# Repaired positions of instruction blocks, ones and loads in the planner, and 64x64 join and U products for the first two groups

## The chip, the cores and the metric

The kernel runs on one core of a Trainium2 chip. The metric is the device time of one launch in microseconds (us), all inputs starting in HBM and the output ending there. The core's engines work in parallel, each through its own list of instructions in order: TensorE (PE; its weight loads are shown apart as PEld), VectorE (DVE), ScalarE (ACT), GpSimd (POOL) and SyncE (SP), which here only issues DMAs. [...]

## The reference

Two stages follow each other. The first is a delta-rule attention over 768 tokens, for 4 batches of 8 heads of 48 features; the second is a gated product on its 3072 x 384 result, without a nonlinear function.

```python
k_n = k / (np.linalg.norm(k, axis=-1, keepdims=True) + 1e-06)
for t in range(S):
    y[:, :, t] = einsum('bhd,bhde->bhe', q[:, :, t], state)
    v_old = einsum('bhde,bhd->bhe', state, k_n[:, :, t])
    state = state + beta_t * einsum('bhd,bhe->bhde', k_n[:, :, t], v[:, :, t] - v_old)
x = y.transpose(0, 2, 1, 3).reshape(B * S, H * D)
out = ((x @ w_a) * (x @ w_b)) @ w_out
```

## The kernel before

**Attention.** The 768 tokens are cut into 24 chunks of 32 (c0 to c23) and six groups of four chunks. Partition p holds token p % 32 of one of four heads, so a "head" in what follows is one of four bands of 32 partitions, and q counts eight such sets: 32 heads in all. For every group there are three parts:

- `prep(g)` squares and sums the keys on ACT and DVE (`sqf`, `ss`, `nm`, `dc`), forms the products of keys with keys and queries on PE (`ga`, 32 matmuls per chunk, tile `bank<-rawb`), copies the key half on ACT for groups 0 and 1 (tile `tt`, there called `kks`), and scales and masks it on DVE (`b`, `at`). It also sums the squares of v and q on ACT (`sqf<-vnb`, `sqf<-rawb`), from which a power of two for the output is made (`sc`).
- `solve(g)` inverts, on DVE, a triangular 32x32 matrix per head, column by column (`tmp<-b,b` and `b<-b,tmp`). For groups 0 and 1 (`HALVES`) it inverts only the two diagonal 16x16 blocks, in 15 such pairs, and PE joins them: 32 matmuls per chunk (`b,tt`, to be called the first join product), a scaled copy on ACT (`wr`), one transposing matmul against the unit matrix (`b,mk`) and 32 more (`wr,xn`, the second join product). ACT copies the result to `tt`.
- `steps(g)` runs through the chunks in turn: the state (`S_ps`) is copied to `sh` (ACT), keys and queries are multiplied with it (`sh,rawb`), DVE subtracts from v (two results `f`, one for even and one for odd heads), PE forms U with the inverse (`f,tt`, 32 matmuls; for c0 it reads v itself, `vnb,tt`), ACT copies it (`u`), and PE updates the state (`S_ps<-u,knb`) and finishes the output rows (`u,at`), which ACT and DVE scale, transpose and split into two f16 halves (`y`, `yt`, `xb`).

Each step of a chunk needs the state of the one ahead, so this is one long chain.

**The gated product** ("MoE" in the code) takes 256 tokens and one of twelve blocks of 128 hidden features at a time: 18 f16 matmuls (`xb,wh`), a copy `a`, a product `g`, two halves `ghl`, and six matmuls with `wo`. A unit of this is the filler that keeps PE busy for most of the span. Its weights come packed; `weights(p)` unpacks a block with three DVE operations (`wh<-late`, `late<-wh`), takes a power of two from its square sum (`sw`), and makes high and low halves. For the first four blocks the low halves are made on PE (`wh,zi` and `wh,neg`), for the rest on DVE.

**What sets the order.** Nothing runs in the order in which the code names it. `Plan` records every operation, and `order()` (lines 413 to 443) lists them by a simulated schedule (`pack`, line 265), with costs in nanoseconds from `price` (line 154); `issue` (line 451) then writes the engines' lists. Into PE's list it puts matmuls on a tile of ones that nobody reads ("fills", line 455) where the plan has PE idle in the first 60 us (`UNTIL`). The plan also models that PE's instructions come in blocks of 256 (`fetch`, line 398): the next block is asked for when one is entered, and comes 3.5 us later, or 5 us while a DMA is under way (`LOADED`). A product of f32 counts as four instructions (two weight loads and two matmuls), one of f16 as two (`op.words`, line 218). The plan before starts counting at block position 0.

**Loads.** SP issues all loads in one queue. Five kinds come first (`EARLY`, line 44). The later ones (`NEXT`, line 45) are held back: POOL copies one element of an earlier tile into the target, so the load waits until the earlier one has landed (line 1056). Names: k (`knb`) and v (`vnb`) are keys and values of two chunks, r (`rawb`) keys and queries laid by feature, b the two small tables beta and masks (`bt`, `mk`), w a weight block (`late`, or `wh` for the third).

**PSUM banks.** Six tiles `bank` are leased by the plan; the last of them serves only the fills until 60 us. ACT and DVE never read a bank at the same time: their reads of one bank follow each other in the planned order.

Of the kernel before, what the change touches and what calls it, by code (L numbers as in the profile page):

```python
# [43 lines left out]
EARLY = [(0, "k"), (0, "b"), (2, "k"), (0, "r"), (2, "r")]  # L44
NEXT = [(0, "v"), (2, "v"), (0, "w"), (1, "w"), (4, "k"), (2, "w"), (4, "r"), (4, "v")]
# [15 lines left out]
class Plan:  # L61
# [92 lines left out]
    def price(eng, name, outs, ins, kw):  # L154
# [36 lines left out]
    def add(self, eng, fn, name, args, kw):  # L191
# [15 lines left out]
        if eng == "SP":  # L207
# [4 lines left out]
            op.move = max(n / 330.0, 20.0)  # L212
# [52 lines left out]
    def pack(self, pri, back=False):  # L265
# [13 lines left out]
        fill = {}  # L279
# [3 lines left out]
        while len(done) < n:  # L283
# [23 lines left out]
            while can[e] and i is None:  # L307
                i = heapq.heappop(can[e])[1]
                if ops[i].words and not back:
                    slip = self.fetch(t, ops[i].words, ops[i].dur if warm else ops[i].cold, pos, come, dma)[0]  # L310
                    if slip > 1.0:
                        heapq.heappush(wait[e], (t + slip, i))
# [29 lines left out]
            if o.words and not back:  # L342
                _, pos, come = self.fetch(t, o.words, o.dur if warm else o.cold, pos, come, dma)
            if e == "PE" and not back:

                if kept:
                    f, took, many = max(free[e], self.SINCE), self.IDLE * (1 if warm else 2), 0
                    while f + took <= t:
# [3 lines left out]
                        took = self.IDLE * (1 if warm else 2)  # L352
                        use, f, many = use + took, f + took, many + 1
                    fill[i] = many
                    if many:
                        f0 = max(free[e], self.SINCE)
                        _, pos, come = self.fetch(f0, 4 * many, f - f0, pos, come, dma)
# [36 lines left out]
    MOVE = (900.0, 1100.0)  # L394
    LOADED = (3500.0, 5000.0)
    IDLE, SINCE, UNTIL = 440.0, 1500.0, 60e3
# [54 lines left out]
    def issue(self, tc):  # L451
        with tc.manual_schedule():
            for i in self.order():
                for _ in range(self.fill.get(i, 0)):
                    self.nc.tensor.matmul(  # L455
                        self.pool[-1][:, 0:256],
                        self.idle,
                        self.idle.unsqueeze(1).broadcast_to([P, 2, P]),
                        start=True,
                        stop=True,  # L460
                        skip_group_check=True,
                    )
# [5 lines left out]
def tile_kernel(ctx, tc, kqt, kn, vn, beta, w, masks, out):  # L468
# [32 lines left out]
    ttr = ring(cst, "tt", 8, [P, 8, 32], F32)  # L501
    wr = ring(cst, "wr", 2, [P, 8, 16], F32)
# [62 lines left out]
    xnt = one("xn", [P, 512])  # L565

# [68 lines left out]
    ats, tts, kks, nms, gnats, zs, vsum = {}, {}, {}, {}, {}, {}, []  # L635
# [23 lines left out]
    acc = [one(f"acc{i}", [P, DM]) for i in range(4)]  # L659

    loaded, whole = set(), set()

    def target(c, what):
        t = {"w": lambda: slots[c].bitcast(F32), "k": lambda: knp(c)[:, 0], "v": lambda: vnp(c)[:, 0], "r": lambda: rawp(c)[:, 0]}
# [18 lines left out]
    def prep(g):  # L683
# [32 lines left out]
        for ci, c in enumerate(chs):  # L716
# [13 lines left out]
            if HALVES[g]:  # L730
                kks[c] = ttr()
                A.copy(kks[c], ga[:, :, 0:32])
# [49 lines left out]
    def solve(g):  # L782
# [35 lines left out]
        for ci, c in enumerate(chs):  # L818
            tts[c] = ttr()
            if HALVES[g]:  # L820
                wp = att()[:, 0:128].rearrange("p (q t) -> p q t", t=16)
                with plan.group():
                    for q, h4, _, _ in heads():
                        T.matmul(
                            wp[tok(h4), q],
                            kks[c][tok(h4), q],
                            XT[tok(h4), 16:32, ci * 8 + q],
                            start=True,
                            stop=True,
                            skip_group_check=True,  # L830
                        )
# [332 lines left out]
```

## Time and profile before

| what | value |
|---|---|
| time, median of 3 runs | 655.7 us (655.66 to 656.97) |
| profiled execution | 655.28 us |
| its span, first to last instruction | 653.3 us |
| mean granted TensorE clock | 0.986 |
| busy: PE, PEld, DVE, ACT, POOL | 632.7, 540.8, 406.4, 271.3, 19.8 us |
| fills on PE (line 455) | 64 matmuls, shown as 128, 33.8 us |
| first matmul of the gated product | 78.59 us from the span's start |

A matmul of f32 stands in the trace as two matmuls and two weight loads; the profile's counts are of these. Busy time of an engine is the time that any of its instructions covers, so 32 overlapping small matmuls count once. In rows of the timeline the columns are start in us, duration in us, engine, line, operation, output and inputs, shape, count, and in brackets the idle time ahead of it and what ended it. In rows of the windows they are the stretch, its length, then busy time and (count of instructions) for PE, PEld, DVE, ACT and POOL, then PE's granted clock, the DMA engines' busy share, and GB/s.

### The profile page before, as it was taken

The page shows a single profiled execution, that of the slowest core. Times are in us where ns is not written, and L with a number is a line of the kernel's source. Part 1 is how long each engine was busy: PE and PEld are TensorE (multiplying, and loading weights), DVE is VectorE, ACT ScalarE, POOL GpSimd, SP SyncE. Part 2 cuts the span into 40 slices and gives each one's busy share as a digit, 9 for nine tenths or more (in the row PEclk, how much of TensorE's full clock was granted, in tenths as well). Part 3 has the DMA queues.
Part 4 walks back from the last instruction along what each step waited for, and adds up shares of the span by engine and source line. Part 5 has one row for each costly group of instructions (what it writes and reads, how often), then busy time and mean ns, then how long its engine had stood idle before and what let it go on. Part 6 is the DMA issues. An engine that isn't in the chain of part 4 may idle for free. (4 is left out here: it accounts for less than half of the span.)

```text
span 653.3 us, 26688 instructions
## 1 busy us (share of the span) xinstructions
PE 632.7 (97%) x12260; PEld 540.8 (83%) x12260; DVE 406.4 (62%) x1059; ACT 271.3 (42%) x599; POOL 19.8 (3%) x33
## 2 busy tenths in 40 slices
PE   8889899999899999999999999999999999999997
PEld 7766678788788888888888888888888888888886
DVE  5958999986665884446884446884447853432222
ACT  3426864465465234332256233255322253332322
POOL 0100000000001000000001000010000000000000
PEclk9969898999999999999999999999999999999999
DMA  7846224025250000043000051000000000000000
GB/s 238 307 171 236 100 76 147 3 87 214 69 189 27 2 22 6 4 141 114 0 27 4 4 205 49 1 27 5 4 2 27 1 27 4 3 26 1 25 1 25
DMA packets 19985, 42.78 MB, mean 65 GB/s; under 512 B 1185, under 2 KB 4513, under 8 KB 19873
## 3 DMA queue, kind: packets, MB, share of 16 engines
q1 hardware_dynamic: 19872, 41.08, 17.9%
q8 instruction: 96, 1.57, 1.0%
q14 instruction: 17, 0.13, 0.1%
HBM read 36.36 MB, written 4.72 MB: 63 GB/s over the span
## 5 line engine op out<-in xcount | busy, mean ns | idle before, releaser
L464 PEld LDWEIGHTS <-wh 128*128 128x128 f16 x2592 | 242.2, 98 | 49.2 <-issue 19.9
L464 PE MATMUL bank<-xb,wh 128*128 128x256 f16 x2160 | 259.4, 273 | 2.3 <-issue 1.6
L464 PE MATMUL bank<-wo,ghl 128*128 128x384 f32 x864 | 189.7, 353 | 0.0
L464 PEld LDWEIGHTS bank<-wo,ghl 128*128 128x128 f32 x864 | 144.4, 190 | 4.0 <-issue 0.6
L464 ACT COPY a<-bank 128x256 f32<-128x256 f32 x144 | 53.5, 372 | 210.5 <-PE bank L464 210.4
L464 DVE TENSOR_TENSOR g<-bank,a 128x256 f32<-128x256 f32 x144 | 61.0, 423 | 117.5 <-ACT a L464 114.8
L464 DVE TENSOR_TENSOR ghl<-g,ghl 128x256 fp32r<-128x256 f32 x144 | 60.9, 423 | 37.4 <-ACT ghl L464 35.0
L464 ACT CAST ghl<-g 128x256 fp32r<-128x256 f32 x144 | 58.2, 404 | 56.6 <-DVE g L464 56.2
L464 PE MATMUL bank<-late,wh 128*128 128x256 f16 x432 | 52.5, 273 | 0.3 <-DVE g L464 0.3
L464 DVE TENSOR_TENSOR b<-b,tmp 128x31 f32<-128x31 f32 (+20 forms) x154 | 49.9, 324 | 3.6
L464 DVE TENSOR_TENSOR tmp<-b,b 128x31 f32<-128x31 f32 (+20 forms) x154 | 49.5, 322 | 3.3
L455 PE MATMUL bank<-ones 128*128 128x256 f32 x128 | 33.8, 421 | 1.1 <-DVE ones L464 1.1
L464 DVE SCALAR_TENSOR_TENSOR y<-bank,sc,y 128x384 f32<-128x384 f32 x23 | 14.2, 617 | 29.2 <-ACT y L464 28.7
L455 PEld LDWEIGHTS bank<-ones 128*128 128x128 f32 x128 | 26.4, 211 | 5.5 <-DVE ones L464 1.1
L464 PE MATMUL bank<-rawb 48*32 48x64 f32 x1280 | 22.9, 219 | 3.4 <-issue 1.9
L464 PEld LDWEIGHTS bank<-rawb 48*32 48x32 f32 x1280 | 19.2, 107 | 8.3 <-issue 4.2
L464 PEld LDWEIGHTS bank<-sh,rawb 48*64 48x64 f32 x1216 | 20.0, 134 | 4.6 <-issue 3.2
L464 ACT COPY sh<-S_ps 112x768 f32<-112x768 f32 x23 | 18.3, 797 | 13.0 <-PE S_ps L464 12.6
L464 PE MATMUL bank<-sh,rawb 48*64 48x48 f32 x1216 | 22.6, 220 | 0.7 <-issue 0.4
L464 PE MATMUL bank<-u,at 32*32 32x48 f32 x1536 | 22.1, 203 | 0.6 <-issue 0.6
L464 PEld LDWEIGHTS bank<-u,at 32*32 32x32 f32 x1536 | 18.5, 105 | 4.6 <-issue 4.0
L464 PEld LDWEIGHTS bank<-f,tt 32*32 32x32 f32 x1472 | 17.4, 105 | 5.9 <-issue 3.4
(115 smaller groups left out, 537.2 us busy)
## 6 DMA issues: line engine op xcount, KB each, us to landing
late<-in_w SPq DMA_DIRECT2D x10, 1152.0 KB, 6.0
rawb<-in_kqt SPq DMA_DIRECT2D x10, 1024.0 KB, 7.8
out<-late SPq DMA_DIRECT2D x24, 192.0 KB, 1.9
knb<-in_kn SPq DMA_DIRECT2D x10, 384.0 KB, 4.5
vnb<-in_vn SPq DMA_DIRECT2D x10, 384.0 KB, 4.7
wh<-in_w SPq DMA_DIRECT2D x2, 1152.0 KB, 5.8
late<-in_kqt SPq DMA_DIRECT2D x2, 1024.0 KB, 6.3
late<-in_kn SPq DMA_DIRECT2D x2, 384.0 KB, 3.3
```

The lines of the kernel that those rows point to most:

```text
L455: self.nc.tensor.matmul(self.pool[-1][:, 0:256], self.idle, self.idle.unsqueeze(1).broadcast_to([P, 2, P]), start=True, stop=True, skip_gr ...
L464: fn(*(self.place(a, lease) for a in args), **{k: self.place(a, lease) for k, a in kw.items()})
```

## The change

Four things are changed.

1. The plan's numbers: blocks of instructions are counted from position 63 (`BEGIN`); a load takes n/400 ns in place of n/330, with 1.2 and 1.3 us around it; a block comes 5.6 us after it is asked for while a DMA is under way; a small PE product whose smaller side is over 32 is priced by its columns or its weights, whichever is longer.
2. The fills: there are now two kinds, the old one of 128x256 and a new one of 32x32 in bf16 (two instructions, planned at 50 ns). The plan tries how many small ones at the front of a gap of over 3 us make the fetch of the block behind it least late, and lets fills end 0.4 us ahead of the operation that they wait for (`SHY`).
3. The loads: k of c0 and c2 first, then r of c0, then the small tables; r of c2 and all later loads wait for the load named beside them.
4. For groups 0 and 1, both join products and U work on 64 partitions: two neighbouring heads stand on the diagonal of a 64x64 weight tile, with zeros beside them, so that 16 matmuls replace 32 (`wides`). The block diagonal is made by `split`: two ACT operations that scale a source by 0 or 1 per partition (`parity`) into the two column halves, in place of one copy. It is used for the key half (formerly `kks`), for the transposed part `xn` (new tile `xtw`, one buffer for all chunks) and for the joined inverse; all live in one tile `tta`, which all groups share. DVE then needs a single `f`: one subtraction over all partitions and one over each odd band of 32, three operations in place of two. `wr` has one buffer in place of two.

```diff
-EARLY = [(0, "k"), (0, "b"), (2, "k"), (0, "r"), (2, "r")]
-NEXT = [(0, "v"), (2, "v"), (0, "w"), (1, "w"), (4, "k"), (2, "w"), (4, "r"), (4, "v")]
+EARLY = [(0, "k"), (2, "k"), (0, "r"), (0, "b")]
+NEXT = [(2, "r", 0, "k"), (0, "v", 0, "r"), (2, "v", 2, "r"), (0, "w", 2, "r"), (1, "w", 0, "v"), (2, "w", 2, "v"), (4, "k", 0, "w"), (4, "r", 1, "w"), (4, "v", 2, "w")]
...
             if min(k, m) <= 64:
+                if min(k, m) > 32:
+                    return max(4 * n / 2.4 + 11.0, 4 * m / 2.4 + 28.0) / (2 if k == 64 else 4)
                 return max(4 * n / 2.4 + 11.0, 56.0) / 4
...
-            op.move = max(n / 330.0, 20.0)
+            op.move = max(n / 400.0, 20.0)
...
-        pos, come = 0, [0.0, 0.0]
+        pos, come = self.BEGIN, [0.0, 0.0]
...
-                    f, took, many = max(free[e], self.SINCE), self.IDLE * (1 if warm else 2), 0
-                    while f + took <= t:
...
+                    f, end = max(free[e], self.SINCE), min(t - self.SHY, slow.get(i, t))
+                    room = end - f
+                    fill[i], best_ = [0, 0], None
+                    for lot in range(int(room / self.IDLE[0]) + 1 if room > 3000.0 else 1):
+                        p_, c_, f_, m = pos, come, f, 0
+                        while f_ + self.IDLE[m >= lot] <= end:
+                            _, p_, c_ = self.fetch(f_, 4 if m >= lot else 2, self.IDLE[m >= lot], p_, c_, dma)
+                            f_, m = f_ + self.IDLE[m >= lot], m + 1
+                        lag = self.fetch(t, 512, 4500.0, p_, c_, dma)[0]
+                        if best_ is None or lag < best_[0] - 1.0:
+                            best_ = lag, lot
...
-    MOVE = (900.0, 1100.0)
-    LOADED = (3500.0, 5000.0)
-    IDLE, SINCE, UNTIL = 440.0, 1500.0, 60e3
+    MOVE = (1200.0, 1300.0)
+    LOADED = (3500.0, 5600.0)
+    BEGIN, IDLE, SINCE, UNTIL = 63, (50.0, 440.0), 1200.0, 60e3
+    SHY, AIM = 400.0, 56
...
+    tta = one("tta", [P, 2048])
+    xtw = ring(cst, "xtw", 1, [P, 8, 64], F32)
+    G.memset(xtw.tiles[0], 0.0)
+
+    def split(dst, src):
+        for i in range(2):
+            A.activation(dst[:, :, 32 * i : 32 * i + src.shape[2]], src, AF.Copy, scale=parity[:, i : i + 1])
+
+    def wides():
+        for q in range(8):
+            for p in range(2):
+                yield q, slice(64 * p, 64 * p + 64), slice(q * D, q * D + D)
...
             if HALVES[g]:
-                kks[c] = ttr()
-                A.copy(kks[c], ga[:, :, 0:32])
+                tts[c] = tta[:, c % 4 * 512 :][:, 0:512].rearrange("p (a b) -> p a b", b=64)
+                split(tts[c], ga[:, :, 0:32])
...
+                for q, r, _ in wides():
+                    T.matmul(
+                        wp[r, q],
+                        tts[c][r, q],
+                        XT[r, 16:32, ci * 8 + q],
...
+            xw = xtw()
+            split(xw, xn[:, :, ci * 8 : ci * 8 + 8].rearrange("p s q -> p q s"))
+            wb_ = wr()
+            A.activation(wb_, wp, AF.Copy, scale=-1.0)
+            plan.behind = {len(plan.ops) - 1}
+            xp = att()[:, 0:256].rearrange("p (q t) -> p q t", t=32)
+            T.matmul(xp, eye, xtv[:, ci], start=True, stop=True, skip_group_check=True)
+            with plan.group():
+                for q, r, _ in wides():
+                    T.matmul(
+                        xp[r, q, 16:32], xw[r, q], wb_[r, q], start=False, stop=True, skip_group_check=True
+                    )
+            split(tts[c], xp)
...
                 fs = [fr(), fr()]
-                for i in range(2):
-                    V.tensor_sub(fs[i], vt, yp[i][:, 0:384])
+                V.tensor_sub(fs[0], vt, yp[0][:, 0:384])
+                if HALVES[g]:
+                    for h4 in 1, 3:
+                        V.tensor_sub(fs[0][tok(h4)], vt[tok(h4)], yp[1][tok(h4), 0:384])
+                else:
+                    V.tensor_sub(fs[1], vt, yp[1][:, 0:384])
...
+                for q, r, cols in wides() if HALVES[g] else ():
+                    T.matmul(up[r, cols], tts[c][r, q], fs[0][r, cols], start=True, stop=True, skip_group_check=True)
```

The instructions move as follows. The first place is PE from its start to the second join product of c0. In these rows the left name is the written tile, then come the inputs, the shape of the result, and how often the row follows itself. Before:

```order
L455 MATMUL bank_66<-ones 128x256 x13
L464 MATMUL bank_61<-rawb 32x64 x32
L464 MATMUL bank_62<-rawb 32x64 x32
L455 MATMUL bank_66<-ones 128x256 x2
L464 MATMUL bank_63<-rawb 32x64 x32
L455 MATMUL bank_66<-ones 128x256 x4
L464 MATMUL bank_64<-rawb 32x64 x32
L455 MATMUL bank_66<-ones 128x256 x28
L464 MATMUL bank_65<-b_3_71,tt_85 32x16 x32
L464 MATMUL bank_61<-b_3_71,tt_86 32x16 x32
L464 MATMUL bank_62<-b_3_71,mk 128x256
L464 MATMUL bank_62<-wr_93,xn 16x16 x32
```

Now (the first two rows shown follow each other 97 times, from PE's start):

```order
L472 LDWEIGHTS ones
L472 MATMUL bank_66<-ones 32x32
L472 MATMUL bank_66<-ones 128x256
L481 MATMUL bank_61<-rawb 32x64 x32
L481 MATMUL bank_62<-rawb 32x64 x32
L481 MATMUL bank_63<-rawb 32x64 x32
L481 MATMUL bank_64<-rawb 32x64 x32
L472 MATMUL bank_66<-ones 128x256 x7
L481 MATMUL bank_65<-sc_120,ones 128x1 x2
L472 MATMUL bank_66<-ones 128x256 x17
L481 MATMUL bank_61<-b_3_71,tta 64x16 x16
L481 MATMUL bank_62<-b_3_71,tta 64x16 x16
```

The 19 large fills ahead of and between the products on `rawb` have become 97 small ones and one large one, the 28 ahead of the join have become 24, and the output's power of two (`sc`) is now made between those.

The second place is ACT in the same stretch, from the root of the key sums on. Before:

```order
L464 ACTIVATE s_121<-ss 128x32
L464 COPY tt_85<-bank_61 128x256
L464 COPY tt_86<-bank_62 128x256
L464 COPY tt_87<-bank_63 128x256
L464 ACTIVATE sqf,sc_129<-vnb 128x768
L464 COPY tt_88<-bank_64 128x256
L464 ACTIVATE sqf,sc_129<-rawb 48x1024 x2
L464 ACTIVATE sqf,sc_129<-vnb 128x768
```

Now:

```order
L481 ACTIVATE s_112<-ss 128x32
L481 ACTIVATE tta<-bank_61,mk 128x8x32 x2
L481 ACTIVATE sqf,sc_120<-vnb 128x768
L481 ACTIVATE tta<-bank_62,mk 128x8x32
L481 ACTIVATE sqf,sc_120<-rawb 48x1024 x2
L481 ACTIVATE tta<-bank_62,mk 128x8x32
L481 ACTIVATE sqf,sc_120<-vnb 128x768
L481 ACTIVATE tta<-bank_63,mk 128x8x32
```

The square of the first v (`sqf,sc<-vnb`) now stands ahead of the copies from the second bank, where it stood behind the third.

The third place is PE behind the first join of c0, up to the state's first use. Before:

```order
L464 MATMUL bank_63<-wr_94,xn 16x16 x32
L455 MATMUL bank_66<-ones 128x256 x6
L464 MATMUL bank_64<-sw_137,ones 128x1
L464 MATMUL bank_65<-sc_129,ones 128x1 x2
L464 MATMUL bank_61<-vnb,tt_89 32x48 x32
L464 MATMUL bank_62<-b_3_71,tt_87 32x16 x32
L464 MATMUL bank_63<-wh,zi 128x384
```

Now:

```order
L481 MATMUL bank_63<-wr_85,xtw_129 64x16 x16
L481 MATMUL bank_64<-b_3_71,tta 64x16 x16
L481 MATMUL bank_65<-vnb,tta 64x48 x16
L481 MATMUL bank_61<-b_3_71,mk 128x256
L481 MATMUL bank_61<-wr_85,xtw_129 64x16 x16
L481 MATMUL S_ps<-u_74,knb 48x48 x32
L481 MATMUL bank_63<-b_3_71,tta 64x16 x16
```

U of c0 (`vnb,tt`, now `vnb,tta`) no longer stands behind six fills and three sums. From there to the gated product's first matmul PE's list holds one large fill now, where it held 11 before.

More of the change, by code (lines that the diff above doesn't have):

```diff
@@ L341, in pack @@
             at[i] = t
-            if o.words and not back:
-                _, pos, come = self.fetch(t, o.words, o.dur if warm else o.cold, pos, come, dma)
             if e == "PE" and not back:
                 if kept:
-                    f, took, many = max(free[e], self.SINCE), self.IDLE * (1 if warm else 2), 0
-                    while f + took <= t:
+                    f, end = max(free[e], self.SINCE), min(t - self.SHY, slow.get(i, t))
[9 more added lines that the diff above has]
+                            best_ = lag, lot
+                    n_small = best_[1]
+                    while True:
+                        k = 0 if fill[i][0] + 1 <= n_small else 1
                         while until <= f:
@@ L351, in pack @@
                             use, until = 0.0, until + self.WINDOW
[L352 to L357, printed above, removed]
+                        took = self.IDLE[k] * (1 if warm or not k else 2)
+                        slip, past, then = self.fetch(f, 2 + 2 * k, took, pos, come, dma)
+                        if slip > 1.0 or f + took > end:
+                            break
+                        use, f, pos, come = use + took, f + took, past, then
+                        fill[i][k] += 1
+                _, pos, come = self.fetch(t, o.words, o.dur if warm else o.cold, pos, come, dma)
                 while until <= t:
@@ L453, in issue @@
             for i in self.order():
[L454 to L462, printed above, removed]
+                for k, n in enumerate(self.fill.get(i, ())):
+                    one = self.idle if k else self.idle.bitcast(BF16)[:, 0:32]
+                    for _ in range(n):
+                        self.nc.tensor.matmul(
+                            self.pool[-1][0 : 32 + 96 * k, 0 : 32 + 224 * k],
+                            one,
+                            one.unsqueeze(1).broadcast_to([P, 1 + k, 32 + 96 * k])[:, 0 : 1 + k],
+                            start=True,
+                            stop=True,
+                            skip_group_check=True,
+                        )
                 for fn, args, kw, lease in self.ops[i].calls:
@@ new lines, in solve @@
+            xw = xtw()
[5 more added lines that the diff above has]
+            T.matmul(xp, eye, xtv[:, ci], start=True, stop=True, skip_group_check=True)
+            with plan.group():
+                for q, r, _ in wides():
+                    T.matmul(
+                        xp[r, q, 16:32], xw[r, q], wb_[r, q], start=False, stop=True, skip_group_check=True
+                    )
@@ L851, in solve @@
+            split(tts[c], xp)
+            yield
         if not HALVES[g]:
```

55 lines of the change are left out of this document (16 added, 39 removed).

## The prediction

> **What bounds the kernel now.** I read the page's busy shares and groups first, then PE's rows in time, then a table of windows.
>
> ```profile
> PE 632.7 (97%) x12260; PEld 540.8 (83%) x12260; DVE 406.4 (62%) x1059; ACT 271.3 (42%) x599; POOL 19.8 (3%) x33
> L455 PE MATMUL bank<-ones 128*128 128x256 f32 x128 | 33.8, 421 | 1.1 <-DVE ones L464 1.1
> ```
>
> PE is busy 97% of the span, but 33.8 us of it are fills, work that nobody reads. The share hides when PE does something useful. The windows tell that better:
>
> ```profile
> 31.10:35.00 3.90, 0.00 (x0) 0.00 (x0) 3.87 (x5) 0.00 (x0) 0.53 (x1) 0.95 0.69 243
> 38.80:44.30 5.50, 5.50 (x15) 4.44 (x15) 0.00 (x0) 1.31 (x3) 0.00 (x0) 0.50 0.74 285
> 78.60:119.00 40.40, 38.61 (x913) 33.31 (x912) 38.11 (x105) 23.65 (x52) 0.00 (x0) 0.96 0.26 91
> 119.00:653.30 534.30, 525.37 (x9817) 454.15 (x9816) 310.49 (x809) 209.69 (x472) 16.79 (x20) 1.00 0.12 41
> ```
>
> From 119 us on PE is busy for 525.4 of 534.3: there a useful matmul costs its full time, and little else counts. In 31.1 to 35.0 PE stands still, in 38.8 to 44.3 it runs fills at clock 0.50. These are PE's rows around both, and the first matmul of the gated product:
>
> ```profile
> 16.61 12.35 PE L455 MATMUL bank<-ones 128*128 128x256 f32 x56
> ...
> 29.19 1.29 PE L464 MATMUL bank<-b,tt 32*32 32x16 f32 x128 [0.23 <-DVE b L464]
> 30.41 0.68 PE L464 MATMUL bank<-b,mk 128*128 128x256 f32 x1
> 35.02 0.79 PE L464 MATMUL bank<-b,mk 128*128 128x256 f32 x1 [3.93 <-issue]
> 35.74 0.74 PE L464 MATMUL bank<-wr,xn 32*16 32x16 f32 x64
> 36.41 1.22 PE L464 MATMUL bank<-b,mk 128*128 128x256 f32 x2
> 37.56 0.71 PE L464 MATMUL bank<-wr,xn 32*16 32x16 f32 x60
> 38.57 0.24 PE L464 MATMUL bank<-wr,xn 32*16 32x16 f32 x4 [0.30 <-issue]
> 38.74 5.49 PE L455 MATMUL bank<-ones 128*128 128x256 f32 x12
> ...
> 45.08 0.88 PE L464 MATMUL bank<-vnb,tt 32*32 32x48 f32 x64
> ...
> 78.59 1.16 PE L464 MATMUL bank<-xb,wh 128*128 128x256 f16 x9
> ```
>
> Until 29.19 PE waits, behind fills, for DVE's solve. From 78.59 the gated product can fill it. So the time is the moment at which PE gets to steady useful work, plus the useful work that is then left.
>
> Both waits above end by "issue", so no engine released them, and the first cuts one matmul in two. From that cut to the second stand 1 + 64 + 2 + 61 passes (60 are shown in the fourth row, one lies in the next), each with a weight load: 256 instructions, which is the plan's block. A block entered at 35.02 was there at 38.57, 3.55 us later; the one entered 256 instructions ahead of the cut, at about 29.2, took 5.8. PE's list has 958 instructions ahead of the cut, and 1024 - 958 = 66, close to the new starting position of 63: the repaired count is right to a few instructions.
>
> [...]
>
> **The change part by part.** The sum is made against the profiled execution, 655.28 us (653.3 of span, 2.0 around it), which lies 0.4 below the median of 655.7.
>
> *Loads, solve and fills, up to the join.* The rows that time the solve before:
>
> ```profile
> 9.55 1.99 PE L464 MATMUL bank<-rawb 48*32 48x64 f32 x128 [1.24 <-DMA rawb<-in_kqt]
> ...
> 12.19 0.29 POOL L464 COPY vnb<-rawb 1x1 f32<-1x1 f32 x2 [11.75 <-DMA rawb<-in_kqt]
> ...
> 15.89 0.84 ACT L464 ACTIVATE sqf<-vnb 128x768 bf16<-128x768 f32 x1 [1.82 <-DMA vnb<-in_vn]
> ...
> 17.52 1.23 DVE L464 STREAM_TRANSPOSE b<-b 128x1024 f32<-128x1024 f32 x1
> 17.69 0.37 ACT L464 COPY tt<-bank 128x256 f32<-128x256 f32 x1 [0.87 <-DVE at L464]
> 17.96 1.06 ACT L464 ACTIVATE sqf<-rawb 48x1024 bf16<-48x1024 f32 x1
> ...
> 19.12 1.05 ACT L464 ACTIVATE sqf<-rawb 48x1024 bf16<-48x1024 f32 x1
> ...
> 27.80 1.25 DVE L464 STREAM_TRANSPOSE b<-b 128x1024 f32<-128x1024 f32 x1
> ```
>
> The first r landed by 9.55, the second by 12.19, and this released the first v, which ACT squared at 15.89. Now the first r releases v, but SP's queue still has the second r ahead of it. The two r came 2.7 us apart for 1024 KB; v has 384 KB, so about 1 us behind the second, at 13. That is 3 us earlier, yet ACT now squares v ahead of the copy from the second bank, and DVE's scaling of that bank waits for the copy: 13 + 1.0 (square and reading its sum) + 0.4 = 14.4. Then come two scalings of v (moved here, 0.5 each) and six operations on banks at 0.4: the transposition starts at 17.7, as before. ACT goes on with three copies of 0.37, four squares at 1.16 and one at 1.0, until 20.8; DVE needs those sums behind three of the fifteen pairs, at about the same time. The sums' further small steps, now inside the solve, cost 0.6; a v scaling moved out spares 0.5. The joined input, ready at 29.05 before, is ready near **29.8**. If v lands an us earlier or later, so does this: the earlier loads give nothing here. Those of the weights landed before DVE was free for them already.
>
> PE's fills can be later than DVE. The sums' two matmuls end near 21.7, then 17 fills follow, 34 passes: at 12.35 / 56 = 0.22 that is 7.5 us. But ahead of the sums PE has idled some 3.5 us, and after the 3.93 us above 12 passes took 5.49, 0.457 each, until 44.3. So up to 15 passes at 0.457 and 19 at 0.22, 11 us, to 32.7. Bounds 29.8 and 32.7; I take **31.5** for the join's start, 2.3 later than before. The 97 small fills have no row; the nearest, 64 small passes over four bands in 0.67, gives 10 to 42 ns for one, at half clock 84, so 1 to 8 us in all, over by the time the first r lands; with v at 13 either end changes nothing.
>
> *From the join to the gated product* PE's list is dense, so its work is the path. Rows that price it, by starts:
>
> ```profile
> 49.18 1.02 PE L464 MATMUL bank<-b,mk 128*128 128x256 f32 x2
> 50.13 0.93 PE L464 MATMUL S_ps<-u,knb 32*48 32x48 f32 x64
> 50.99 0.88 PE L464 MATMUL bank<-u,at 32*32 32x48 f32 x64
> ...
> 55.03 1.15 PE L464 MATMUL bank<-sh,rawb 48*64 48x48 f32 x64
> 56.10 0.91 PE L464 MATMUL bank<-wh,zi 128*128 128x384 f32 x2
> ...
> 59.45 0.81 PE L464 MATMUL bank<-wh,zi 128*128 128x384 f32 x2
> 60.19 0.88 PE L464 MATMUL bank<-f,tt 32*32 32x48 f32 x64
> 60.89 0.74 PE L464 MATMUL bank<-wr,xn 32*16 32x16 f32 x64
> 61.56 0.44 PE L464 MATMUL bank<-wo,negr 128*128 128x384 f32 x1
> L464 PEld LDWEIGHTS bank<-sh,rawb 48*64 48x64 f32 x1216 | 20.0, 134 | 4.6 <-issue 3.2 <-DVE g L464 0.8 <-DVE sw L464 0.2
> ```
>
> U and a join product take 0.7 (60.19 to 60.89 to 61.56). No 64x64 group is in this trace. The nearest is `sh,rawb`: 32 matmuls with 64 weight columns, over all four quadrants of the array, in 1.07, thus 8 per quadrant at 134 ns, the mean of its weight loads. A new group has 16 matmuls on two quadrants, again 8 each: **1.07**. Below: the old 0.7, if half the matmuls outweigh the wider weights. Above: 16 x 0.134 = 2.14, if the two quadrants do not overlap. I take 1.07, as the weights have that row's width.
>
> The list holds ten such groups (10.7), four transposing matmuls (0.95, 3.8 in all), two state updates (1.7), two `sh,rawb` (2.1), two `u,at` (1.7), eleven `wh,zi` (0.74, 8.1), eight `wh,neg` and three `wo,negr` (some 2), five sums and one fill (1.4): 31.5. Following the lists of ACT and DVE beside it, most inputs are there in time; PE waits some 2 us late in the stretch for `zi`, which DVE makes behind its unpacking, and the six block edges need 21 to 35 us at 3.55 to 5.8 each, so 1 more. The gated product starts at 31.5 + 34.5 = **66**, 12.6 us earlier. Two things that were done by 78.59 are then still to do, U of c2 and one `wh,zi` with its sum: -1.6.
>
> *Behind it* 14 more 64x64 groups follow, each 0.37 dearer on a full PE: -5.2. Fewer instructions spare part of the 1.8 us that PE idled in 78.6 to 119 and of a few later edges: +1. DVE has one more `f` for seven chunks:
>
> ```profile
> L464 DVE TENSOR_TENSOR f<-vnb,bank 128x384 f32<-128x384 f32 x38 | 19.9, 546 | 3.0 <-PE bank L464 2.8
> L464 DVE SCALAR_TENSOR_TENSOR wh<-late,wh 128x1152 int32<-128x1152 int32 x14 | 18.8, 1350 | 0.1
> ```
>
> That is 7 x 0.5 = 3.5 us on an engine that is busy for 38.11 of 40.4 us there; I put 1 us of it on PE's path (below 0, above 3.5). ACT gets four more operations a chunk of at most 0.37 each, 1.5 us; outside the join, PE's other work covers it, and without that cover 8 chunks would cost 12. The single `wr` and `xtw` and the shared `tta` make a chunk wait for PE's product just ahead; the next chunk's products cover this. Sum: 12.6 - 1.6 - 5.2 + 1 - 1 = 5.8 gained, 655.3 - 5.8 = **649.5**.
>
> **The rivals.** *A 64x64 group costs the old 0.7.* Then 24 x 0.37 = 8.9 less: 640.6. For it: half the matmuls. Against it: 134 ns a weight load. Chance 0.08.
>
> *DVE takes the bound.* At its first gated matmul the new order leaves DVE's list some 9 us short of where it stood at 78.6 (four unpacking operations of 1.35 and low halves of blocks 4 and 5), so DVE is only about 3 us ahead of before, with 3.5 more to do; PE would give its lead back in waits: 655. For it: 38.11 of 40.4. Against it: 310 of 534 behind 119, and PE has gated units to do until then. Chance 0.17.
>
> *Slower: the edge moves instead of going.* By the repaired count, edges now lie at the end of the fourth `rawb` product, in the second join product of c0, in the first state update, and on. If a block is late inside the join, PE loses 3.9 us and some 5 more cold, as up to 44.3: 658.5. It decides once a wait is long enough for clock 0.50, which 3.93 was and 0.30 was not. For it: six blocks of 5.8 us are 35 us, in 34. Against it: fewer instructions per us. Chance 0.14.
>
> [...] Chance 0.07.
>
> **How the numbers follow.** The forecast, 649.5 with 644 to 654 as its own range, has 0.51; 0.03 is left for what I have not seen. About 0.2%, 1.3 us, is what a measurement of this kernel can tell from no change. Faster: 0.51, 0.08 and half of DVE's case, 0.67. Same: the other half and a little, 0.10. Slower: 0.23. The range leaves out the dear end of the last rival and reaches to the cheap groups: 640 to 660.
>
> **What would show it.** The join's first product at 30 to 33; 64x64 groups 1.07 apart; no "issue" wait of PE over 2 us between the join and the gated product; that one near 66; the joined input no earlier than before. I am wrong if v lands by 11.5 (then all is earlier), if a group takes 2.1 (all later), or if PE idles over 5 us in the 40 us behind its first gated matmul.

## The result and the profile after

The changed kernel took 665.3 us (median of four runs, 664.9 to 667.9), the kernel before, beside it on the same chip, 656.3. The ratio is 1.012 with a 95% interval of 1.009 to 1.015: slower by 1.2%. The forecast was 649.5. The profiled execution took 665.42 us, with a span of 663.3, 10.0 more than before. Ratios in this text leave out a run that lies over 1.5% above the fastest of its kernel; where a kernel's runs spread that far, this favours it, and the median of all of them is given too.

The page of the changed kernel, PE's busy line and the granted clock in 40 slices:

```profile
PE 642.2 (97%) x11513; PEld 551.4 (83%) x11513; DVE 411.1 (62%) x1066; ACT 284.9 (43%) x631; POOL 21.0 (3%) x35
...
PEclk9957998959999999998999999999999999999999
```

The trace has 747 fewer PE matmuls, and yet PE is busy for 9.5 us more. Its share of the span is the same 97%. What differs is the clock: two dips, in slices 3 and 4 and around slice 9.

Start of the changed kernel, rows of PE, ACT and DVE in time:

```profile
13.50 0.84 ACT L481 ACTIVATE sqf<-vnb 128x768 bf16<-128x768 f32 x1 [0.75 <-DMA vnb<-in_vn]
18.07 1.22 DVE L481 STREAM_TRANSPOSE b<-b 128x1024 f32<-128x1024 f32 x1
21.58 7.58 PE L472 MATMUL bank<-ones 128*128 128x256 f32 x34
29.41 2.04 PE L481 MATMUL bank<-b,tta 64*64 64x16 f32 x64 [0.24 <-DVE b L481]
31.38 1.11 PE L481 MATMUL bank<-b,mk 128*128 128x256 f32 x2
32.42 1.56 PE L481 MATMUL bank<-wr,xtw 64*64 64x16 f32 x32
33.81 1.88 PE L481 MATMUL bank<-b,tta 64*64 64x16 f32 x32
35.51 1.93 PE L481 MATMUL bank<-vnb,tta 64*64 64x48 f32 x32
37.37 1.22 PE L481 MATMUL bank<-b,mk 128*128 128x256 f32 x2
...
57.60 1.13 PE L481 MATMUL bank<-f,tta 64*64 64x48 f32 x32
58.67 0.91 PE L481 MATMUL bank<-wh,zi 128*128 128x384 f32 x2
...
71.11 1.15 PE L481 MATMUL bank<-xb,wh 128*128 128x256 f16 x9
```

No row of the join is preceded by an "issue" wait, so the stop of 3.93 us is gone. (`b,mk` is the product called transposing above. It multiplies X by the unit matrix and only reorders its columns; nothing is transposed.) The first two 64x64 groups take 2.04 us together, 1.02 each. From 33.8 the same group takes 1.88, and at 57.6 a group starts 1.07 before its successor again. The gated product starts at 71.1, 7.5 us earlier than before, but 5 later than forecast.

PE in windows of 10 us, of the changed kernel (the stretch, its length, PE's busy time and instructions, granted clock, DMA share, GB/s):

```profile
30.00:40.00 10.00, 10.00 (x178) 0.64 0.47 148
40.00:50.00 10.00, 10.00 (x208) 0.50 0.61 218
50.00:60.00 10.00, 10.00 (x151) 0.66 0.42 146
100.00:110.00 10.00, 8.90 (x222) 0.83 0.01 2
130.00:140.00 10.00, 10.00 (x141) 0.59 0.05 5
140.00:150.00 10.00, 10.00 (x184) 0.50 0.30 116
150.00:160.00 10.00, 10.00 (x189) 0.88 0.02 4
```

and those of the kernel before in which its clock was under full:

```profile
30.00:40.00 10.00, 5.77 (x189) 0.73 0.75 269
40.00:50.00 10.00, 9.92 (x156) 0.76 0.29 110
70.00:80.00 10.00, 9.48 (x305) 0.83 0.02 4
90.00:100.00 10.00, 8.21 (x337) 0.97 0.40 131
100.00:110.00 10.00, 10.00 (x130) 0.86 0.64 227
```

This is the main reading of the case. In the join of the first group (30 to 60 us) and that of the second (130 to 160), PE is busy all the time, waits for nothing, and runs at half clock. Counting busy time times (1 - clock) as lost, the changed kernel loses 12.0 us in the first stretch, 10.3 in the second and 1.5 at 100: 23.8. A dip from 309.33 to 312.74 adds up to 1.7. The kernel before loses 7.2 in its five rows and nothing more until 650 us. The difference, 16.6 to 18.3, is more than the 10.0 by which the span grew. Without it the change would be 6.6 to 8.3 us faster; the forecast sum was 5.8. This counting is an upper estimate, since not all of PE's rows halve with the clock (`b,mk` went from 1.11 to 1.22 only).

### The profile page after: what moved, and what is told of

Read it like the earlier page. It is cut to its first block, busy times and chain, and to the rows that moved or that the text cites. A ratio compares the mean times of both kernels' runs of the same rounds, so it can differ in the third digit from the quotient of the medians.

```text
span 663.3 us, 25228 instructions
## 1 busy us (share of the span) xinstructions
PE 642.2 (97%) x11513; PEld 551.4 (83%) x11513; DVE 411.1 (62%) x1066; ACT 284.9 (43%) x631; POOL 21.0 (3%) x35
## 3 DMA queue, kind: packets, MB, share of 16 engines
q1 hardware_dynamic: 19872, 41.08, 17.7%
## 5 line engine op out<-in xcount | busy, mean ns | idle before, releaser
L481 PE MATMUL bank<-rawb 48*32 48x64 f32 x1280 | 26.4, 243 | 5.3 <-DMA rawb<-in_kqt 4.3
L481 PEld LDWEIGHTS bank<-rawb 48*32 48x32 f32 x1280 | 23.1, 124 | 9.7 <-DMA rawb<-in_kqt 5.1
L481 ACT COPY sh<-S_ps 112x768 f32<-112x768 f32 x23 | 18.3, 796 | 18.9 <-PE S_ps L481 18.8
L481 DVE TENSOR_TENSOR f<-vnb,bank 128x384 f32<-128x384 f32 (+1 forms) x45 | 23.7, 548 | 3.3 <-PE bank L481 2.6
L481 PEld LDWEIGHTS bank<-f,tta 32*32 32x32 f32 (+1 forms) x1248 | 20.1, 112 | 4.6 <-issue 3.7
L481 PE MATMUL bank<-f,tta 32*32 32x48 f32 (+1 forms) x1248 | 23.1, 208 | 0.0
```

What stands on the lines that cost most here:

```text
L481: fn(*(self.place(a, lease) for a in args), **{k: self.place(a, lease) for k, a in kw.items()})
```

## The experiments

The theory after this result: 64x64 products on the diagonal, though they keep PE busy, count as too little work, and the clock falls. The rivals: any unbroken run of small products does this, whatever its form; or it comes from elsewhere (block edges, other engines).

### One part of the change at a time

The plan's numbers, fills and loads of the change, with the products of before:

```diff
-            with plan.group():
-                for q, r, _ in wides():
-                    T.matmul(wp[r, q], tts[c][r, q], XT[r, 16:32, ci * 8 + q], ...)
+            with plan.group():
+                for q, h4, _, _ in heads():
+                    T.matmul(wp[tok(h4), q], kks[c][tok(h4), q], XT[tok(h4), 16:32, ci * 8 + q], ...)
```

(and so for the second join product and U).

> The changed kernel's planner numbers, loads and fills with the 32x32 products of before in the first two groups. Theory 1 (the 64x64 form cools the clock): granted clock 1.00 from about 34 to 56 us and 1.00 between 127 and 152 us, first gated matmul at 63 to 68 us, time 646 to 651 us, faster than before. Theory 2 (the joins, standing together without fills or gated products between, cool it in any form): 0.50 in both stretches, first gated matmul near 71, time 660 to 666 us. Theory 3 (block edges of the new order): an idle of 3 us or more put down to issue in the first 80 us, time near 656.

And the reverse, the products of the change with the plan's numbers, fills and loads of before:

```diff
-        pos, come = self.BEGIN, [0.0, 0.0]
+        pos, come = 0, [0.0, 0.0]
...
-    BEGIN, IDLE, SINCE, UNTIL = 63, (50.0, 440.0), 1200.0, 60e3
+    IDLE, SINCE, UNTIL = 440.0, 1500.0, 60e3
...
```

(the price of a 64-wide product stays that of the change).

> The planner numbers, loads and fills of before, with the 64x64 products of the change (and their price in the planner). Theory 1: granted clock 0.50 in the stretches in which 64x64 groups stand together, 20 us or more of it in all, time 662 to 672 us, slower than before. Theory 2: what counts is whether fills or gated products stand between; where the old numbers keep them between, 1.00, time 645 to 655 us. Theory 3 (block edges and loads of the new planner numbers cost the time, not the products): time 648 to 654 us, faster than before by the fewer instructions.

With the old products: 652.7 us against 658.2 for the kernel before beside it, ratio 0.991 (0.988 to 0.995). With the new products alone: 666.8, ratio 1.013 (1.009 to 1.018). So the whole loss comes with the products and the operations of ACT and DVE that belong to them, and the repaired numbers by themselves gain 0.9%. The first is a little above the 646 to 651 that was expected, the second inside its 662 to 672. The same two windows of PE in the changed kernel, then with the old products, then with the new products alone:

```profile
34.00:56.00 22.00, 22.00 (x337) 0.50 0.67 228
120.00:150.00 30.00, 28.62 (x416) 0.70 0.12 41
```

```profile
34.00:56.00 22.00, 20.45 (x555) 0.92 0.64 226
120.00:150.00 30.00, 29.39 (x906) 1.00 0.18 56
```

```profile
34.00:56.00 22.00, 22.00 (x403) 0.53 0.51 181
120.00:150.00 30.00, 28.01 (x352) 0.74 0.24 81
```

The clock follows the products, not the plan. The 0.92 is one dip, from 38.14 to 41.55, behind a wait of 1.10 us. Both kernels are planned anew, so their order differs too, and this pair alone does not say what about the products counts.

### What cools the clock: forms and columns by themselves

A small kernel runs one form at a time on PE alone, behind 40 full products 128x256 each time:

```diff
+    def wide(c, k, src, full=0):
+        for _ in range(c):
+            for q in range(8):
+                for p in range(2):
+                    r = slice(64 * p, 64 * p + 64)
+                    mm(r, r, src[r, 64 * (q % 2) : 64 * (q % 2) + 64], k)
+            if full:
+                warm(full)
```

> A small kernel that leaves out the whole computation (it writes zeros and scratch): nine stretches of one form of f32 product each, on TensorE alone, with 40 products 128x256 (17 to 18 us) ahead of each. In order: 64x64 on the diagonal with 16 moving columns (320 products), the same with half of the weights zero, the same with 48 columns, 32x32 in four bands with 16 columns (896), the same with 48, 64x64 in all four quadrants with 16 columns (320), 128x128 with 16 columns (160), and 64x64 on the diagonal with 16 columns with one, then with two products 128x256 behind each 16 of them. Theory 1 (the 64x64 diagonal form, bound by its weight loads, counts as too little work): granted clock falls to 0.50 in stretches 1 to 3, stays above 0.9 in the 32x32 stretches 4 and 5, and in 8 and 9 it stays near 1.00. Theory 2 (any unbroken run of small products cools it): 0.50 in stretches 1 to 7, near 1.00 only in 8 and 9. Theory 3 (the cold came from something else in the kernel, such as other engines' work or a block edge): near 1.00 in all nine. Price: 1.03 to 1.07 us for 16 products 64x64 at full clock, about 0.67 us for 32 products 32x32.

Windows of PE inside seven of the nine stretches, in this order: 64x64 with 16 columns, the same with half the weights zero, with 48 columns, 32x32 with 16, 64x64 on four quadrants with 16, 128x128 with 16, and 64x64 with 16 and one full product behind each group:

```profile
32.00:52.00 20.00, 20.00 (x380) 0.50 0.01 2
84.00:100.00 16.00, 16.00 (x305) 0.50 0.01 3
124.00:140.00 16.00, 16.00 (x556) 1.00 0.02 4
164.00:204.00 40.00, 20.44 (x1389) 0.50 0.02 5
304.00:312.00 8.00, 7.76 (x284) 0.50 0.02 4
340.00:396.00 56.00, 56.00 (x264) 0.50 0.00 1
424.00:440.00 16.00, 16.00 (x324) 1.00 0.01 3
```

Both theories fall as I had put them. It is not the 64x64 form: in whole 128x128 products with 16 columns the clock was 0.50 as well, with PE busy for 56.00 of 56.00 us. (The 32x32 row is no clean test: PE was busy for only 20.44 of 40.00 us and waited for "issue" in between, mostly 1.83 us at a time, so its cold may be that of idle time. The same holds for 32x32 with 48 columns, busy for 3.05 of 4.00 us at 0.50 from 244 and for 3.12 of 8.00 us at 1.00 from 256.) And it is not any unbroken run of small products: 64x64 with 48 columns stayed at 1.00. Zeros in half of the weights changed nothing: 0.50 with and without. With one full product behind each group the clock stayed at 1.00, and with two as well (8.00 us busy of 8.00 at 1.00, from 464). What the cold rows above share is the number of moving columns per weight load, 16. The theory was therefore put anew: what counts is the time in which columns stream through the array, not the time in which PE is taken.

A second small kernel varies the columns and asks what brings the clock back, with two stretches that follow a cold one directly:

```diff
+    ('wide', 24, 24, 'rnd'),
+    ('wide', 24, 32, 'rnd'),
+    ('wide', 24, 40, 'rnd'),
+    ('wide', 24, 16, 'rnd'), ('wide', 40, 32, 'rnd', 'on'),
+    ('wide', 24, 16, 'rnd'), ('wide', 40, 48, 'rnd', 'on'),
+    ('narrow', 28, 48, 1),
+    ('whole', 160, 48),
```

> A small kernel that leaves out the whole computation, like the one on forms. Stretches in order: 64x64 on the diagonal with 24, 32 and 40 moving columns (24 groups of 16 each), each behind 40 products 128x256; then with 16 columns and, straight behind it without a warm stretch, 40 groups with 32; then with 16 and, straight behind, 40 groups with 48; then 32x32 with 48 columns and one product 128x256 behind each 32; then 128x128 with 48 columns (160). Theory 1 in the form that the first small kernel left it (what counts is the time in which moving columns stream, not the time in which TensorE is taken): with full clock at 48 and half at 16, 40 stays at 1.00, 24 falls to 0.50, 32 is open. Straight behind a cold stretch 48 columns bring the clock back within some 8 us, 32 do so only if they also hold it. 128x128 with 48 columns, three times the streaming of the 16 that were at 0.50, stays near 1.00. If instead the count of columns has nothing to do with it and the earlier stretch with 48 was warm by chance, 24, 32 and 40 all fall to 0.50.

Windows of PE, in this order: 64x64 with 24, 32 and 40 columns; 32 columns straight behind the cold stretch; 48 columns likewise; 128x128 with 48:

```profile
32.00:56.00 24.00, 24.00 (x455) 0.50 0.01 3
84.00:100.00 16.00, 16.00 (x556) 1.00 0.02 4
124.00:136.00 12.00, 12.00 (x420) 1.00 0.02 4
212.00:260.00 48.00, 48.00 (x905) 0.50 0.01 2
332.00:360.00 28.00, 28.00 (x968) 1.00 0.02 4
456.00:508.00 52.00, 52.00 (x246) 0.50 0.00 1
```

and two rows of its timeline, 24 groups each:

```profile
79.77 22.59 PE L37 MATMUL bank<-rnd 64*64 64x32 f32 x768
119.75 22.59 PE L37 MATMUL bank<-rnd 64*64 64x40 f32 x768
```

With 24 columns the clock fell to 0.50, with 32 it held 1.00; behind a cold stretch 32 did not bring it back, 48 did. And the columns from 32 to 40 were free at full clock: both took the same 0.94 us a group (22.59 us for 24). The last window is a miss: 128x128 with 48 columns was expected near 1.00. It shows that columns per weight load are not the measure by themselves, since 48 held the clock for 64x64 (1.00) and not for 128x128 (0.50). The stretch between these two, 32x32 with 48 columns and one full product behind each group, stayed at 1.00, with PE busy for 34.11 of 40.00 us from 388.

The share of time in which columns stream can be estimated from this. A fill of 256 columns takes two passes of the 0.22 us in the row at 21.58, so one column 1.7 ns. A group of 64x64 products is 8 products on each of two quadrants, taken to stream side by side: 24 columns stream 8 x 24 x 1.7 = 0.33 of 0.94 us, 35%; 32 columns 47%. 128x128 with 48 columns ran its first 3.4 us, to about 450.3, at 1.00, some 15 products, and streamed 36% before the clock fell. Between fall and hold lies a row of the first small kernel, 64x64 with 16 columns and one full product behind each group:

```profile
418.14 1.11 PE L37 MATMUL bank<-rnd 64*64 64x16 f32 x32
419.18 0.70 PE L41 MATMUL bank<-rnd 128*128 128x256 f32 x2
419.81 1.11 PE L37 MATMUL bank<-rnd 64*64 64x16 f32 x32
```

It streams 0.22 + 0.44 of 1.67 us, 40%, and kept 1.00 for all of its 16 rounds. So behind a warm stretch the clock fell at 35 and 36% and held at 40 and 47%. At half clock a group took 1.6 to 1.7 us. If a column takes twice as long there, as a pass of the fill did (0.457 us against 0.22), 32 columns stream for 52 to 55% of it, which wasn't enough to return; 48 columns, about 80%, were.

The join can be judged by the same estimate. A chunk in the changed kernel has two groups of 16 columns (0.22 us of columns each, in 1.05), the transposing product (0.44 in 1.11) and U (0.65 in 1.13): 1.53 of 4.34 us, 35%. Before, with groups of 0.7 and U of 0.7 to 0.88, it was 1.53 of 3.2 to 3.4, 45 to 48%. The 64x64 products have exactly as many columns per quadrant as the 32x32 ones (8 x 16 a group), but hold PE for 1.05 us in place of 0.7.

One thing more stands in all twelve traces: the stretches at one clock that begin and end inside the run last a whole multiple of 3.41 us, in those of the experiments to the 0.1 us that windows of 4 us tell (30.7 and 20.5 us in the first small kernel, nine times and six times). In the changed kernel half clock was granted from 32.85 to 56.74 (seven times that), 104.53 to 107.94 (once), 131.84 to 152.32 (six times) and 309.33 to 312.74 (once). So the clock changed in steps of 3.41 us here, and a share that is averaged over a chunk of 4.3 us is only a guide to what a step holds.

### The test in the kernel: more columns, same order

If this holds, the changed kernel can be cured by columns that nobody needs. The 64x64 join products get 32 columns in place of 16; every other instruction and the order stay as they are (in the traces, too, the rows of each engine follow each other as in the changed kernel):

```diff
-            wp = att()[:, 0:128].rearrange("p (q t) -> p q t", t=16)
+            wp = att()[:, 0:256].rearrange("p (q t) -> p q t", t=32)
...
-                        XT[r, 16:32, ci * 8 + q],
+                        XT[r, 0:32, ci * 8 + q],
...
-            xp = att()[:, 0:256].rearrange("p (q t) -> p q t", t=32)
+            xk = att().rearrange("p (k q t) -> p k q t", k=2, t=32)
+            xp = xk[:, 0]
...
-                        xp[r, q, 16:32], xw[r, q], wb_[r, q], ...
+                        xk[r, :, q, 16:32], xw[r, q], wb_[r, q].unsqueeze(1).broadcast_to([64, 2, 16]), ...
```

> The changed kernel, instruction for instruction in the same order, with 32 instead of 16 moving columns in the 64x64 products of the joins (the first half of X, and a second copy of the correction, written beside the wanted part and read by nobody). A 64x64 product with 16 columns takes as long as one with 48 in the small kernel at full clock (140 against 144 records in 4 us), so at an unchanged clock it costs nothing. Theory 1 (too few moving columns cool the clock): granted clock above 0.9 for most of 34 to 56 us and of 130 to 152 us, first gated product at 60 to 64 us, time 640 to 650 us; if 32 columns are only just enough or not enough, the cold stretches get shorter or stay, 655 to 666 us. Theory 2 (the run of products without fills or gated ones between, whatever they stream): clock as in the changed kernel, 663 to 668 us.

The ratio to before is 0.990 (0.986 to 0.994); the changed kernel's was 1.012. With twice the columns in its join products the kernel is some 2% faster than without (0.990 / 1.012). Over all twelve runs the median is 653.8 against 657.9 before (0.994), from 646.9 to 661.2, and the time broadly follows the clock: 646.9 at a mean clock of 1.00, 653.1 (the profiled run) at 0.984, 661.2 at 0.971. Order, fills, loads and the extra operations of ACT and DVE are those of the changed kernel, so none of them is the loss by itself. The expected 640 to 650 was missed, and so was the start of the gated product at 60 to 64: it came at 68.56. The two windows:

```profile
34.00:56.00 22.00, 20.57 (x468) 0.84 0.67 229
120.00:150.00 30.00, 28.61 (x598) 1.00 0.12 42
```

The second stretch is cured. In the first a dip is left from about 46 to 53 us, behind a wait of 1.39 us for "issue": in keeping with the small kernel, where 32 columns held the clock at 1.00 and did not bring it back from 0.50.

The same padding in one group at a time tells the two stretches apart:

```diff
+            n_ = 32 if g == 0 else 16
+            wp = att()[:, 0 : 8 * n_].rearrange("p (q t) -> p q t", q=8)
```

> The changed kernel in the same order of instructions, with 32 moving columns in the joins of the first group of chunks alone; the second group's joins keep 16. Theory 1 (each join with 16 columns loses its own cold stretch): the clock falls to 0.50 between about 120 and 150 us only; of the some 14 us between the changed kernel and the one padded in both groups, the first group's stretch gives 4 to 8, time 657 to 662 us. If the second group's cold stretch came from the first one's lateness (another order of arrival, not its columns), it goes too, and the time is that of the kernel padded in both, near 651.

> The same with 32 moving columns in the joins of the second group alone; the first group's keep 16. Theory 1: 0.50 from about 34 to 56 us as in the changed kernel, 1.00 from 127 to 152 us, 8 to 11 us faster than the changed kernel, time 654 to 658 us. If the second stretch is a matter of the gated products that come too late and not of the columns, it stays cold and the time stays at 663 to 666.

First the kernel with the first group padded, then with the second:

```profile
34.00:56.00 22.00, 21.70 (x580) 1.00 0.73 253
120.00:150.00 30.00, 29.64 (x470) 0.60 0.12 42
```

```profile
34.00:56.00 22.00, 22.00 (x365) 0.50 0.58 191
120.00:150.00 30.00, 28.61 (x536) 1.00 0.12 43
```

Each group's columns decide its own stretch and not the other's. The first group padded: ratio 1.001 (0.998 to 1.005), median 657.2, at the low end of the expected 657 to 662. The second: ratio 0.996 (0.993 to 0.999), profiled execution 656.3, as expected, but over all its runs the median is 659.6, with six of twelve at 662 to 668. Those have a lower mean clock (0.95 to 0.96) and no profile; where they lost it is open.

### Trying to make the clock sturdier

48 columns in the first of the two products (three copies of the wanted 16):

```diff
-            wp = att()[:, 0:128].rearrange("p (q t) -> p q t", t=16)
+            wp = att()[:, 0:384].rearrange("p (k q t) -> p k q t", k=3, t=16)
...
-                        XT[r, 16:32, ci * 8 + q],
+                        XT[r, 16:32, ci * 8 + q].unsqueeze(1).broadcast_to([64, 3, 16]),
```

> The kernel padded in both groups, with 48 instead of 32 moving columns in the first of the two products of a join (three copies of the wanted 16; the second product keeps 32). In the small kernel 48 columns not only hold the full clock but bring it back from half, which 32 do not. Theory 1: after a wait the clock comes back sooner, so the time is 0 to 4 us under that of the kernel with 32, 646 to 652 us, with less spread between runs. If only the holding matters, the same time within 1 us.

A miss: median 658.6, ratio 0.999 (0.995 to 1.002), and the profile has half clock from about 45 to 56 us (46 to 53 with 32), and a short dip at 104 (0.65 from 104 to 108). It ran on another chip than the kernel with 32, so the two compare by their ratios only. Changing one of the two products is not enough to bring the clock back, or something else varies between these runs; this is open.

Two kernels add full products of ones, in the bank that takes the transposing product. Their sums are disturbed by it, so they do not compute the reference; the instructions are otherwise the same and in the same order. The first leaves 16 columns and adds two such products per chunk:

```diff
+            fn, args, kw, lease = plan.ops[-1].calls[-1]
+            plan.ops[-1].calls += [(fn, (xk[:, 1].rearrange("p q t -> p (q t)"), ones,
+                                         ones.unsqueeze(1).broadcast_to([P, 2, P])), kw, lease)] * 2
```

> The changed kernel in the same order with 16 moving columns as it stands, and in each of the eight joins two extra products 128x256 of ones behind the one that X takes, into columns of the same bank that nobody reads: 16 products of 0.44 us, 7 us more work for TensorE. Theory 1 (moving columns streamed hold the clock): 1.00 or short dips in 34 to 56 and 130 to 152 us, so that work added makes the kernel faster than the changed one by 4 to 10 us: 655 to 661 us. If the 64x64 form itself is what cools it, or the place of the joins: 7 us slower, 670 to 674 us.

```profile
34.00:56.00 22.00, 21.84 (x498) 1.00 0.64 217
120.00:150.00 30.00, 28.61 (x393) 0.72 0.12 41
```

Half of what was expected. In the first group the 64x64 products with 16 columns ran at 1.00, so neither their form nor their place by itself made the clock 0.50. In the second group it fell all the same, and the time is 667.7 (ratio 1.012, 1.006 to 1.017), no gain over the changed kernel. By the estimate above, two join groups, a transposing product and two fills are 1.8 us of columns in 4.1, 43%, and 46% with U beside them: more than the 40% that held in the small kernel. So the average over a chunk does not decide by itself. The clock fell at 127.29, came back for one step at 130.71 and fell again from 134.12 to 147.77. The step ahead of the first fall, 123.88 to 127.29, holds part of a wait of 1.28 us for DVE, and PE is busy for 2.59 of its 3.41 us. The join of the first group has no such wait. That this wait tips the step is likely; it was not tried, and the second fall is not explained.

The second adds one such product per chunk of the first group to the kernel padded with 32 columns:

```diff
+            if g == 0:
+                plan.ops[-1].calls.append((fn, (xk[:, 1]..., ones, ...), kw, lease))
```

> The kernel padded to 32 columns in both groups, with one extra product 128x256 in each of the first group's four joins (1.8 us of work), in the same order. Its profile with the padding alone had a wait of 1.39 us at 44 us and half the clock from 46 to 53 behind it, and its runs spread from 647 (clock 1.00 throughout) to 661. Theory 1: the extra full products bring the clock back after such a wait, fewer runs above 655, median 648 to 653 us. If such dips come from elsewhere, the same spread, 2 us later.

The dip at 46 us is gone from its profile (no window from 32 to 160 us is under 1.00), but the spread is not: the median of its twelve runs is 659.0, from 647.4 to 665.8; the ratio of 0.991 (0.987 to 0.995) rests on the four fastest alone. The expected median was 648 to 653, so the dip in the first join isn't what sets the spread. What does is open. Whether the steps of 3.41 us fall on other instructions from run to run was not tested.

The steadiest of the faster versions is the first experiment's: the repaired plan with 32x32 products, 649.3 to 653.9 in six runs, ratio 0.991, faster than the kernel before and than the changed one.

## Why the prediction was wrong

**What held.** v landed by 13.50 (13 forecast) and the transposition started at 18.07 (17.7), so the earlier loads gave nothing at the join. A 64x64 group took 1.02 to 1.07 at full clock (1.07). The stop of 3.93 us went and no edge took its place: the longest "issue" wait of PE between join and gated product was 0.23 us. DVE did not become the bound: in the 40 us behind the first gated matmul PE waited 0.8 us for it and 0.2 for "issue". The blocks are real: in the small kernel 32x32 products came in lots of 256 instructions,

```profile
162.22 1.90 PE L37 MATMUL bank<-rnd 32*32 32x16 f32 x128 [2.49 <-issue]
165.95 1.90 PE L37 MATMUL bank<-rnd 32*32 32x16 f32 x128 [1.83 <-issue]
```

one every 3.73 us, 3.45 at three edges of twelve (128 matmuls and as many weight loads), close to the 3.55 that the prediction read from two waits. So PE waited at the edges there, 1.55 to 1.83 us at most of them, and no run shows blocks that cost nothing, for which the prediction had 0.07.

**What was off but small.** The join started at 29.41, not 31.5: I had allowed for up to 15 of 34 passes of the fills at half clock, and all ran at full (7.58 / 34 = 0.22).

**What failed** is the term "31.5 us of work" between join and gated product, and with it the "14 more 64x64 groups, each 0.37 dearer". Both were priced from rows at clock 1.00, as if an engine that works is an engine at full clock; half clock inside the join was put at nothing. From 29.41 to 71.11 the list took 41.7 us, not 34.5; up to 12.0 of it went at the half clock of 30 to 60 us. Without these it is 29.7, so the work itself was sized about right. The further groups were to cost 5.2; the second join alone lost 10.3 to the clock. I had looked for the clock only behind idle time, and the window that I quoted at 0.50 stood behind a stop of 3.93 us, which seemed to say the same. What I did not ask is what a stretch without any full products streams. The counts were in the rows: the join's products keep their 16 columns a weight load, while each takes a weight load twice as wide.

The plan has the same blind spot: `price` takes the longer of columns and weights for a 64-wide product, and `op.use`, from which the plan reckons whether PE is warm, adds that whole price. So it sees the join as fully warm. What it compares with is near to what the runs show by the estimate above: it counts PE as warm still over 43% of 3.413 us, where the clock fell at 35 and 36% and held at 40% in the small kernels, and as warm again over 75%, where it stayed cold at 52 to 55% and came back at about 80% (line 363 of the new kernel).

**The rivals.** None named this mechanism. The slower one, with an edge inside the join, ended on the right side for another reason: no block was late there (the longest "issue" wait was 0.23 us). The slower cases had 0.23 together, and the range stopped at 660.

## What to carry to other kernels

Price a stretch of small products twice: by the time that PE is held, and by the columns that it streams in that time. In the small kernels the clock fell where the second was 35 or 36% of the first, and held at 40%; in the kernel 43 to 46% went both ways. So the guess from these runs is half the clock there or below, whatever the busy share says (it was 22.00 of 22.00 us), and that it stays so until denser work comes: 48 columns brought it back, 32 did not in over 60 us. Fewer, wider products that hold PE longer per column can lose by this what they save in instructions, as here (ratio to before 1.012 with them, 0.991 with the 32x32 ones under the same numbers, fills and loads); beside a 64-wide weight load 32, 40 and 48 columns took the same 0.94 us a group, and 32 held the clock at 1.00.

## What the runs showed of the hardware that was not expected

- The granted clock was 0.50 with PE busy 22.00 us of 22.00 and no wait in it; with 16 or 24 columns a weight load in 64x64 products it fell, in the small kernels within 6 us behind a stretch at 1.00 (22.93 to 27.74 us with 16, 73.26 to 78.94 with half the weights zero, 22.63 to 27.1 with 24).
- The clock changed in steps: stretches at one clock lasted whole multiples of 3.41 us (3.41, 20.48 and 23.89 us at 0.50 in the changed kernel).
- It took more to return than to hold: 32 columns held 1.00 (16.00 us of 16.00 from 84), and stayed at 0.50 for over 60 us where they followed a cold stretch (48.00 us of 48.00 from 212), while 48 came back to 1.00 (28.00 us of 28.00 from 332).
- At full clock a group of 64x64 products took 0.94 us with 32, 40 or 48 columns (18.87 us for 20 groups with 48).
- The transposing product `b,mk` took 1.11 us at full clock and 1.22 at half, the fill of the same 128x256 shape 0.44 at full. Its moving operand is read in another order than it lies in; whether that is the reason wasn't tried.
